# Attention scores from a split in natural layout, in six 64-row matmuls for each step, and the last 64 keys in plain float32

## The chip, the cores and the metric

One core of a Trainium2 chip runs the whole program in one launch. The metric is the device time of one execution in microseconds (us). The kernel before took 601.89 us (median of three runs, 601.4 to 602.93).

## What is computed

```python
def _attn_ref(q, k, v):                       # 4 batches, 12 heads, 448 tokens, 64 columns
    S = q.shape[2]
    scale = 1.0 / np.sqrt(q.shape[-1])
    scores = scale * np.matmul(q, k.transpose(0, 1, 3, 2)) - np.log(S)
    attn = 1.0 / (1.0 + np.exp(-scores))      # a sigmoid: no sum over the keys
    return np.matmul(attn, v)

# x: the heads side by side, 1792 tokens x 768
# soft mixture of 8 experts with 4 slots each: logits = x @ phi; a softmax over the tokens weighs
# the slots' inputs, relu(slots @ w1[e]) @ w2[e] follows, a softmax over the slots weighs the outputs
# last layer: h = x @ w_in (float64 weights); g = h * cos(h); out = g @ w_out (float64 weights)
```

All inputs but `w_in` and `w_out` are float32.

## The kernel before, in words

The program has three stages: attention with the routing, the experts, and the last layer. Only the first is changed.

The attention goes through 24 pairs of heads (`NP`; six pairs make a batch). Head 0 of a pair lies in rows 0 to 63 of its tiles, head 1 in rows 64 to 127; queries are columns 0 to 447 of `raw`, keys columns 448 to 895. A pair has four **steps** g: three with 128 keys and one with the last 64. The loop over `slots` writes each engine's instructions out by hand, in this order: `scores(i, g)` on TensorE into a tile of two PSUM banks (`ps_s`, two tiles in turn), `squash` (the sigmoid, ScalarE), then `attn_v` for the step two before (`LAG`), then one item of `todo` (transposes of finished tokens, logits, sums of the routing), then what VectorE has to prepare for the next pair. `in_between` fills VectorE with work that nothing waits for at once, by the budgets of `SPARE`: the routing's exponentials (`slow`) and the narrowing of `w_in` from float64 patterns to float32 (`narrow`, four instructions for each of 24 pieces of 512 columns).

A float32 score needs three float16 products: upper keys with upper queries, lower keys with upper queries, upper keys with lower queries. Before, `hi` holds four blocks. In blocks 2 and 3 the upper and lower keys of one head lie one under the other in 128 rows, and in blocks 0 and 1 that head's upper queries stand twice, so one 128-row matmul gives the first two products of a head; a 64-row matmul for each head adds the third:

```python
rows = [(slice(0, P), j) for j in range(2)] + [(top, 0), (bottom, 1)]
```

To bring the parts into place VectorE does a cast (L279), three copies in `cast_keys` (L285 to L287) and three in `cast_queries` (L292, L293) for each pair, and GpSimd (POOL) two subtractions (L280, L281). The last 64 keys of both heads go through one product of 128 rows: `split_v` (VectorE, L254, L255) makes two float32r parts of v on a block diagonal, `split_a` (ScalarE L261, POOL L262) two parts of the weights, and three float32r matmuls (L350) take the place of a float32 one. The very last pair does it in float32 without a split (L347).

SyncE issues every DMA in the order of the code: `load_v` and `load_qk` at g = 1, halves of weights (`load_half`) at g = 2, g = 3 and in most pairs at g = 1. There are 15 slots for weights; more is loaded as pieces of `w_in` are narrowed. After the attention its memory is used again from the first address on, in slots of 8,192 bytes per partition: `a0`, `a1`, `a2`, `ct`, `m4`, `zone`. A load into one waits until what lay there has been used. In order of address the attention's pools are `xt2p`, `rawp`, the even pair's `hi` and `lo`, its v, `vh` and `vl`, the odd pair's `hi` and `lo`, its v, `ap_` (the weights), `xtp`, `xp` (the turned tokens), `midp` (the routing's small tiles).

Of the kernel before, what the change touches and what calls it, by code (L numbers as in the profile page):

```python
# [9 lines left out]
F16 = mybir.dt.float16  # L10
# [10 lines left out]
NP = B * HP  # L21
# [11 lines left out]
# a pair's v: three columns of blocks for each head, and one that the two share  # L33
VW = 7 * D
# slots for half a chunk of weights: from the start on, and after the attention for w_out too
W_SLOTS, A_SLOTS = 15, 3
# so many of the first ones are loaded after the attention as well
LATE = 1
# columns of w_in that become float32 at a time, and how many times a pair of heads
CV = 512  # L40
RATE = 1.15
# how far the attention's second product is behind the first
LAG = 2
# steps of a pair of heads that load half a slot, beside every third and fourth
EXTRA = [(i, 1) for i in range(2, 22)]
# steps between the slots' weights and their use
PAUSES = 5
# microseconds that VectorE has in each of a pair's steps for what nothing waits for
SPARE = 0.4, 0.4, 0.8, 1.0
# the difference of the biases of float64 and float32, 1023 - 127, in the upper eight bits of eleven  # L50
F64_SCALE = 2.0 ** -112
# 2^f for f from -1/2 to 1/2, the powers from the first on
# [7 lines left out]
def fused(ctx: ExitStack, tc: tile.TileContext, qk, vv, phi, w1, w2, w_in, w_out, out):  # L60
# [24 lines left out]
    def own_logits(b):  # L85
        """A batch's, tokens to rows; the last one's where no slots' sums are any more."""
        if b < B - 1:
            return l_all[0:CT, b]
        return s_acc.rearrange("p a f -> p (a f)")[0:CT, DM - P:].rearrange("p (c s) -> p c s", c=NC_T)

    # the weights in the order in which they are used, and where each goes
# [8 lines left out]
    # the work space is filled for the first group of experts, after others that are free sooner  # L100
# [6 lines left out]
    def load_half():  # L107
        """A load of weights in two, that it holds up what the attention needs for less long."""
        if not halves_left:
            halves_left.extend(load_w(2))  # L110
        halves_left.pop(0)()
# [45 lines left out]
    def narrow(a, words, dst, eng=None):  # L157
        """float64 bit patterns (low word, high word) to the float32 of their leading bits."""
        low, high = words[:, :, 0], words[:, :, 1]
        # as a float32, the high word has eight of the eleven bits of the exponent in its own exponent;  # L160
        # less the difference of the biases, what three places to the left are a float32's magnitude is left
# [16 lines left out]
    def exp_weights(pool, b, l):  # L178
        """Softmax over the slots (its maximum is taken off), as [hi, lo, hi, lo] for float32r."""
# [30 lines left out]
    # ------------------------------------------------------------ attention and routing  # L210
    with ExitStack() as at:
        # from the first that is free at the end to the last
# [4 lines left out]
        vp = at.enter_context(tc.tile_pool(name="vp", bufs=1))  # L217
        vh, vl = [vp.tile([P, P], F32R, name=f"v{x}") for x in "hl"]
# [10 lines left out]
        # ahead of what is needed for longer  # L229
        midp.tile([P, S], F32, tag="lc", name="lc")  # L230
# [4 lines left out]
        def load_qk(i):  # L235
            # the second pair's before the first's are done with, where no tokens lie yet
            pool, tag = (xp, "xtok") if i == 1 else (rawp, "raw")
            raw[i] = pool.tile([P, QK], F32, tag=tag, name=f"raw{i}", bufs=2 if i == 1 else 1)
            # the first pair's in two, that the first half is there sooner
            for k in (1, 0) if i == 0 else ():  # L240
                nc.sync.dma_start(out=raw[i][:, k * S:(k + 1) * S], in_=qk[i, :, k * S:(k + 1) * S])
            if i:
                nc.sync.dma_start(out=raw[i], in_=qk[i])
# [5 lines left out]
        def split_v(i):  # L249
            """The last 64 rows of two heads, each in its own block, in two parts for float32r."""  # L250
            for j in range(2):
                js = slice(j * D, (j + 1) * D)
                v = v32[i][js, 6 * D:]
                nc.vector.tensor_copy(vh[js, js], v)  # L254
                nc.vector.tensor_sub(vl[js, js], v, vh[js, js].bitcast(F32))  # L255

        def split_a(i):
            """The last of a pair's weights in two parts for float32r."""
            one = aa[i, 3]
            a = aa[i, 3] = ap_.tile([P, 2, S], F32R, tag="a", name=f"ar{i}")  # L260
            nc.scalar.copy(a[:, 0], one)  # L261
            nc.gpsimd.tensor_sub(a[:, 1], one, a[:, 0].bitcast(F32))  # L262

        def block(i, k):
            """Queries of two heads, then keys of two heads."""
            return hi[i][:, k * S:(k + 1) * S]

        def new_pair(i):
            hi[i] = pairs[i % 2].tile([P, 4 * S], F16, tag="hi", name=f"hi{i}")
            lo[i] = pairs[i % 2].tile([P, S], F16, tag="lo", name=f"lo{i}")  # L270
# [3 lines left out]
        def cast(i):  # L274
            """Both heads' upper parts where only one of them stays, and what the keys' leave."""
            new_pair(i)
            r = raw.pop(i)
            both = hi[i].rearrange("p (a k s) -> p a k s", a=2, k=2)
            nc.vector.tensor_copy(both[:, :, 0], r.rearrange("p (a s) -> p a s", a=2))  # L279
            nc.gpsimd.tensor_sub(block(i, 1), r[:, S:], block(i, 2))  # L280
            nc.gpsimd.tensor_sub(lo[i], r[:, 0:S], block(i, 0))  # L281

        def cast_keys(i):
            """The lower part of each head's keys under its upper one."""
            nc.vector.tensor_copy(block(i, 3)[bottom], block(i, 2)[bottom])  # L285
            nc.vector.tensor_copy(block(i, 2)[bottom], block(i, 1)[top])  # L286
            nc.vector.tensor_copy(block(i, 3)[top], block(i, 1)[bottom])  # L287

        def cast_queries(i):
            """Each head's upper part of the queries twice."""  # L290
            for half in (top, bottom):
                nc.vector.tensor_copy(block(i, 1)[half], block(i, 0)[bottom])  # L292
            nc.vector.tensor_copy(block(i, 0)[bottom], block(i, 0)[top])  # L293

        def first_casts():
            new_pair(0)
            q, k = raw[0][:, 0:S], raw.pop(0)[:, S:]
            nc.vector.tensor_copy(block(0, 2)[top], k[top])
            nc.scalar.copy(block(0, 3)[bottom], k[bottom])
            nc.vector.tensor_sub(block(0, 2)[bottom], k[top], block(0, 2)[top])  # L300
            nc.scalar.copy(block(0, 0)[top], q[top])
            nc.vector.tensor_copy(block(0, 0)[bottom], q[top])
            nc.scalar.copy(block(0, 1)[bottom], q[bottom])
            nc.vector.tensor_sub(lo[0][top], q[top], block(0, 0)[top])  # L304
            nc.scalar.copy(block(0, 1)[top], q[bottom])
            nc.gpsimd.tensor_sub(lo[0][bottom], q[bottom], block(0, 1)[bottom])
            nc.vector.tensor_sub(block(0, 3)[top], k[bottom], block(0, 3)[bottom])

        def scores(i, g):
            """The keys' two parts with the queries' upper one, then the upper part with the lower."""  # L310
            ps = ps_s.tile([P, 2, 512], F32, tag="sc", name=f"sc{i}_{g}")
            rows = [(slice(0, P), j) for j in range(2)] + [(top, 0), (bottom, 1)]
            # the very first of them head by head, as they come
            for at, j in rows if i or g else rows[0::2] + rows[1::2]:
                upper = at.stop - at.start == P
                keys, q = block(i, 2 + j)[at], block(i, j) if upper else lo[i][at]
                if g < 3:
                    o, kk = ps[:, j, 0:S], keys[:, g * P:(g + 1) * P]
                else:
                    o, kk = ps[j * D:(j + 1) * D, 0, 0:S], keys[:, g * P:g * P + D]  # L320
                nc.tensor.matmul(o, kk, q, start=upper, stop=not upper)  # L321
# [15 lines left out]
        def attn_v(i, g):  # L337
# [3 lines left out]
            for j in range(2):  # L341
# [4 lines left out]
                elif i == NP - 1:  # L346
                    nc.tensor.matmul(av[i][js, 0:S], v32[i][js, 6 * D:], a[js], start=False, stop=True)  # L347
            if g == 3:
                for v, x in ((vh, 0), (vl, 0), (vh, 1)) if i < NP - 1 else ():
                    nc.tensor.matmul(av[i][:, 0:S], v, a[:, x], start=False, stop=x == 1)  # L350
# [8 lines left out]
        def route(i):  # L359
            """Tokens of one pair of heads to rows; logits once a batch has all its pairs."""  # L360
# [13 lines left out]
            if hp == 2:  # L374
                # ahead of what waits, that there is room for the next pair
# [4 lines left out]
            if hp == HP - 1:  # L380
# [3 lines left out]
                else:  # L384
                    # something that the array has left to do while the maximum is on its way
# [5 lines left out]
        def logits(b, half):  # L391
            """Three pairs of heads side by side, each in its own columns of the array."""
# [8 lines left out]
        def warm_up(n, what=ident):  # L401
            """Products for nothing, that the array's clock is up when something comes."""
# [727 lines left out]
```

## Time and profile before

| | |
|---|---|
| median of three runs | 601.89 us |
| span of the profiled execution | 601.1 us |
| busy in the span: TensorE (PE), VectorE (DVE), ScalarE (ACT), POOL | 544.4, 410.4, 291.6, 140.8 us |
| moved by DMA | 98.14 MB, 162 GB/s on average over the span |
| attention, experts, last layer | about 0 to 226, 226 to 305, 305 to 601 us |

The profile lists one execution. The time of the runs also holds what lies around the span. A matmul's duration in the rows includes the time in which it drains; how fast a series runs is read from one start to the next. PEclk is the granted clock of TensorE as a share of full speed: 1.0 is 2.4 GHz, 0.5 is 1.2 GHz, and a value between is a mean over both. The chain of waits and the waits of an engine tell what it stood still for.

### The profile page before, as it was taken

The page shows a single profiled execution, that of the slowest core. Times are in us where ns is not written, and L with a number is a line of the kernel's source. Part 1 is how long each engine was busy: PE and PEld are TensorE (multiplying, and loading weights), DVE is VectorE, ACT ScalarE, POOL GpSimd, SP SyncE. Part 2 cuts the span into 40 slices and gives each one's busy share as a digit, 9 for nine tenths or more (in the row PEclk, how much of TensorE's full clock was granted, in tenths as well). Part 3 has the DMA queues.
Part 4 walks back from the last instruction along what each step waited for, and adds up shares of the span by engine and source line. Part 5 has one row for each costly group of instructions (what it writes and reads, how often), then busy time and mean ns, then how long its engine had stood idle before and what let it go on. Part 6 is the DMA issues. An engine that isn't in the chain of part 4 may idle for free.

```text
span 601.1 us, 8006 instructions
## 1 busy us (share of the span) xinstructions
PE 544.4 (91%) x2943; PEld 327.4 (54%) x2943; DVE 410.4 (68%) x786; ACT 291.6 (49%) x471; POOL 140.8 (23%) x114
## 2 busy tenths in 40 slices
PE   8999898979898999777988777888999999999997
PEld 3332223223232353222246565656999999999996
DVE  5899989798999822410039999997655655565553
ACT  5877656655665731100036666645444544444442
POOL 3444424323343300000017566561000000000000
PEclk8999989889898999997999989999999999999999
DMA  6688786773642499999974343302000200020002
GB/s 198 212 300 295 250 279 220 243 256 121 216 162 89 168 318 384 386 385 375 348 263 158 105 151 113 130 28 92 1 0 1 93 0 1 1 93 0 1 1 93
DMA packets 46247, 98.14 MB, mean 163 GB/s; under 512 B 2944, under 2 KB 17664, under 8 KB 46208
## 3 DMA queue, kind: packets, MB, share of 16 engines
q1 hardware_dynamic: 46208, 97.63, 47.1%
q8 instruction: 23, 0.38, 0.3%
q14 instruction: 16, 0.13, 0.1%
HBM read 92.11 MB, written 5.51 MB: 162 GB/s over the span
## 4 chain that ended last, share of the span: by engine, by line
PE 54%; DVE 33%; DMA 4%; issue 4%; SPq 3%; ACT 1%; DVEq 0%; ACTq 0%
PE o L1005 29%; PE sc L321 7%; PE av L345 6%; DVE wf L169 5%; DVE wi L965 4%; DMA w<-in_w 4%; SPq L142 3%; DVE hi L285 2%; PE h L746 2%; DVE hi L286 2%; DVE wf L172 2%; PE av L350 2%; DVE hi L292 2%; DVE wi L172 2%; PE h L951 2%
## 5 line engine op out<-in xcount | busy, mean ns | idle before, releaser
L1005 PE MATMUL o<-gh,wh 128*128 128x448 f32 x384 | 128.9, 367 | 10.2 <-ACT gh L989 9.0
L1005 PE MATMUL o<-gh,wl 128*128 128x448 f32 x384 | 131.4, 374 | 2.7 <-POOL wl L910 2.6
L1005 PE MATMUL o<-gl,wh 128*128 128x448 f32 x384 | 129.7, 369 | 2.5 <-POOL gl L990 2.4
L332 ACT ACTIVATE a<-sc,bias_s 128x896 f32<-128x896 f32 x96 | 87.7, 914 | 63.5 <-PE sc L321 58.8
L975 ACT ACTIVATE wi<-wi 128x448 f32<-128x448 f32 x64 | 37.0, 578 | 108.3 <-DVE wi L970 76.0
L1005 PEld LDWEIGHTS o<-gh,wh 128*128 128x128 f32 x384 | 71.1, 188 | 19.3 <-ACT gh L989 12.4
L1005 PEld LDWEIGHTS o<-gh,wl 128*128 128x128 f32 x384 | 72.7, 192 | 13.4 <-POOL wl L910 7.8
L1005 PEld LDWEIGHTS o<-gl,wh 128*128 128x128 f32 x384 | 72.0, 190 | 11.4 <-POOL gl L990 7.0
L321 PEld LDWEIGHTS <-hi 64*128 64x128 f16 (+3 forms) x384 | 21.8, 99 | 100.1 <-issue 73.7
L345 PE MATMUL av<-a,v 128*64 128x448 f32 x288 | 74.3, 596 | 0.0
L321 PE MATMUL sc<-hi 128*128 128x448 f16 x192 | 52.3, 381 | 17.0 <-DVE hi L293 15.5
L990 DVE TENSOR_TENSOR gl<-wi,gh 128x448 fp32r<-128x448 f32 x49 | 31.9, 651 | 42.8 <-ACT gh L989 42.8
L981 DVE TENSOR_TENSOR wi<-h,wi 128x448 f32<-128x448 f32 x64 | 39.7, 621 | 29.0 <-ACT wi L975 29.0
L953 ACT ACTIVATE wi<-h 128x448 f32<-128x448 f32 x64 | 34.6, 541 | 21.6 <-PE h L951 21.3
L262 POOL TENSOR_TENSOR ar<-a,ar 128x448 fp32r<-128x448 f32 x23 | 28.4, 1235 | 66.2 <-ACT ar L261 66.2
L910 POOL TENSOR_TENSOR wl<-wf,wh 128x768 fp32r<-128x768 f32 (+2 forms) x17 | 33.3, 1958 | 36.6 <-ACT wh L906 36.6
L280 POOL TENSOR_TENSOR hi<-raw,hi 128x448 f16<-128x448 f32 x23 | 25.9, 1126 | 56.9 <-DVE hi L279 40.4
L989 ACT CAST gh<-wi 128x448 fp32r<-128x448 f32 x64 | 35.8, 560 | 5.6 <-DVE wi L981 5.4
L321 PE MATMUL sc<-lo,hi 64*128 64x448 f16 x192 | 37.2, 381 | 0.3 <-DVE lo L304 0.3
L788 PE MATMUL so<-w,zone 128*32 128x512 f32 (+1 forms) x256 | 27.6, 523 | 8.6 <-DMA w<-in_w 8.6
L970 DVE TENSOR_TENSOR wi<-wi 128x448 f32<-128x448 f32 x48 | 30.0, 625 | 1.7
L169 DVE SCALAR_TENSOR_TENSOR wf<-wo,wf 128x768 uint32<-128x768 uint32 x16 | 29.4, 1836 | 0.5
(176 smaller groups left out, 713.1 us busy)
## 6 DMA issues: line engine op xcount, KB each, us to landing
w<-in_w SPq DMA_DIRECT2D x25, 1024.0 KB, 14.3
w<-in_w SPq DMA_DIRECT2D x44, 512.0 KB, 6.9
wi<-in_w_in SPq DMA_DIRECT2D x24, 512.0 KB, 6.6
wo<-in_w_out SPq DMA_DIRECT2D x16, 768.0 KB, 4.3
raw<-in_qk SPq DMA_DIRECT2D x23, 448.0 KB, 3.3
v<-in_vv SPq DMA_DIRECT2D x24, 224.0 KB, 3.6
out_t<-wi SPq DMA_DIRECT2D x24, 224.0 KB, 2.1
zone<-in_w SPq DMA_DIRECT2D x1, 1024.0 KB, 8.5
```

The costliest lines, as they stand in the source:

```text
L169: lambda: nc.vector.scalar_tensor_tensor(out=t, in0=low, scalar=29, in1=t, op0=ALU.logical_shift_right, op1=ALU.bitwise_or),
L321: nc.tensor.matmul(o, kk, q, start=upper, stop=not upper)
L332: nc.scalar.activation(a, ps, AF.Sigmoid, bias=bias_s, scale=qk_scale)
L345: nc.tensor.matmul(av[i][js, 0:S], v32[i][:, vc:vc + D], a[:, j], start=g == 0, stop=False)
L910: nc.gpsimd.tensor_sub(wl[:, f, cols], wf[f][:, cols], wh[:, f, cols].bitcast(F32))
L953: nc.scalar.activation(ph, h, AF.Copy, bias=0.25, scale=inv2pi)
L970: nc.vector.tensor_sub(ph, tn, ph)
L975: nc.scalar.activation(tn, ph, AF.Sin, scale=-2.0 * math.pi)
L981: nc.vector.tensor_mul(g, hs.pop(u), tn)
L989: nc.scalar.copy(gh, g)
L990: (nc.gpsimd if u < NF - 1 else nc.vector).tensor_sub(gl, g, gh.bitcast(F32))
L1005: nc.tensor.matmul(ps, w[:, f, o * P:(o + 1) * P], g, start=f == 0 and w is wh and g is gh, stop=f == NF - 1 and g is gl,)
```

## The change

Parts are split where they lie. `hi` and `lo` are two tiles of the shape of `raw` (896 columns each); head 0 stays in the upper 64 rows, head 1 in the lower. One cast and one subtraction on VectorE fill them, at g = 0 and g = 1. Each step's scores are six 64-row matmuls, the three products for head 0 and head 1 in turn. The last 64 keys go through two float32 matmuls of 64 rows by 64 columns in all pairs. `split_v`, `split_a`, `cast_keys`, `cast_queries` and POOL's part of the splits are gone. The first instruction of a piece of `w_in` is always VectorE's (before, ScalarE did 22 of 24), and `SPARE` is larger. Comments that were taken out are not shown.

```diff
-SPARE = 0.4, 0.4, 0.8, 1.0
+SPARE = 0.8, 0.4, 1.3, 1.2
...
-        vp = at.enter_context(tc.tile_pool(name="vp", bufs=1))
-        vh, vl = [vp.tile([P, P], F32R, name=f"v{x}") for x in "hl"]
...
         def new_pair(i):
-            hi[i] = pairs[i % 2].tile([P, 4 * S], F16, tag="hi", name=f"hi{i}")
-            lo[i] = pairs[i % 2].tile([P, S], F16, tag="lo", name=f"lo{i}")
+            hi[i] = pairs[i % 2].tile([P, QK], F16, tag="hi", name=f"hi{i}")
+            lo[i] = pairs[i % 2].tile([P, QK], F16, tag="lo", name=f"lo{i}")
...
+        def cast_upper(i):
             new_pair(i)
+            nc.vector.tensor_copy(hi[i], raw[i])
+        def cast_lower(i):
+            nc.vector.tensor_sub(lo[i], raw.pop(i), hi[i])
         def first_casts():
+            nc.vector.tensor_copy(hi[0][:, k], r[:, k])
+            nc.scalar.copy(hi[0][:, q], r[:, q])
+            nc.vector.tensor_sub(lo[0][:, k], r[:, k], hi[0][:, k])
+            nc.vector.tensor_sub(lo[0][:, q], r[:, q], hi[0][:, q])
         def scores(i, g):
             ps = ps_s.tile([P, 2, 512], F32, tag="sc", name=f"sc{i}_{g}")
+            h, l = hi[i], lo[i]
+            terms = [(h, h), (l, h), (h, l)]
+            for n, (keys, q) in enumerate(terms):
+                for j, at in enumerate((top, bottom)):
+                    o = ps[:, j, 0:S] if g < 3 else ps[j * D:(j + 1) * D, 0, 0:S]
+                    kk = keys[at, S + g * P:min(S + (g + 1) * P, QK)]
+                    nc.tensor.matmul(o, kk, q[at, 0:S], start=n == 0, stop=n == len(terms) - 1)
...
-                elif i == NP - 1:
+                else:
                     nc.tensor.matmul(av[i][js, 0:S], v32[i][js, 6 * D:], a[js], start=False, stop=True)
...
-                if g == 3 and i < NP - 1:
-                    split_a(i)
-                if g == 0 and due(i):
-                    narrow_piece(None)
...
-                if more and g in (1, 2):
-                    (cast_keys, cast_queries)[g - 1](i + 1)
...
-                if more and g == 0:
-                    cast(i + 1)
-                if i < NP - 1 and g == 3:
-                    split_v(i)
+                if more and g < 2:
+                    (cast_upper, cast_lower)[g](i + 1)
```

TensorE, the step g = 1 of the second pair and the product for the first pair's last keys. Before (`sc` are the scores, `ar` the split weights, `vh` and `vl` the parts of v):

```order
L321 LDWEIGHTS hi_179
L321 MATMUL sc_1_246<-hi_179 128x448
L321 LDWEIGHTS hi_179
L321 MATMUL sc_1_246<-hi_179 128x448
L321 LDWEIGHTS hi_179
L321 MATMUL sc_1_246<-lo_180,hi_179 128x448
L321 LDWEIGHTS hi_179
L321 MATMUL sc_1_246<-lo_180,hi_179 128x448
L350 MATMUL av_208<-ar_220,vh 128x448
L350 MATMUL av_208<-ar_220,vl 128x448
L350 MATMUL av_208<-ar_220,vh 128x448
```

The same place now:

```order
L279 LDWEIGHTS hi_169
L279 MATMUL sc_1_228<-hi_169 128x448
L279 LDWEIGHTS hi_169
L279 MATMUL sc_1_228<-hi_169 128x448
L279 LDWEIGHTS lo_170
L279 MATMUL sc_1_228<-hi_169,lo_170 128x448
L279 LDWEIGHTS lo_170
L279 MATMUL sc_1_228<-hi_169,lo_170 128x448
L279 LDWEIGHTS hi_169
L279 MATMUL sc_1_228<-lo_170,hi_169 128x448
L279 LDWEIGHTS hi_169
L279 MATMUL sc_1_228<-lo_170,hi_169 128x448
L305 MATMUL av_195<-a_3_207,v_137 64x448 x2
```

Two 128-row and two 64-row matmuls became six of 64 rows, head 0 and head 1 in turn, and three matmuls over both heads became two over one head each.

VectorE, the work for one pair. Before (`sl` are sums for the slots):

```order
L279 CAST hi_883<-raw_829 128x2x448
L169 SCALAR_TENSOR_TENSOR wi<-wi_1_1_381,wi 128x512
L285 COPY hi_883<-hi_883 64x448
L286 COPY hi_883<-hi_883 64x448
L287 COPY hi_883<-hi_883 64x448
L519 COPY s_acc<-sl_0_904 128x384
L519 COPY run_z<-sl_0_904 128x1
L172 SCALAR_TENSOR_TENSOR wi<-wi_1_1_381,wi 128x512
L292 COPY hi_883<-hi_883 64x448 x2
L293 COPY hi_883<-hi_883 64x448
```

Now:

```order
L256 CAST hi_990<-raw_934 128x896
L163 TENSOR_SCALAR wi<-wi_2_1_459 128x512
L168 TENSOR_SCALAR wi<-wi 128x512
L259 TENSOR_TENSOR lo_991<-raw_934,hi_990 128x896
L169 SCALAR_TENSOR_TENSOR wi<-wi_2_1_459,wi 128x512
L172 SCALAR_TENSOR_TENSOR wi<-wi_2_1_459,wi 128x512
```

The copies are gone, one subtraction has come, and a piece of `w_in` begins on VectorE.

SyncE, the loads into the attention's own memory at its end, with what each waits for (engines, and DMAHW for earlier loads; `w_1_1_1` goes to `a0`, `w_1_2_0` to a slot for weights, then `a1`, `a2`, `ct`, `m4`, `zone`). Before:

```order
L130 DMA w_1_2_0_2311<-in_w 128x4x512 [waits DVE_49,Activation_49]
L130 DMA w_1_2_1_2313<-in_w 128x4x512 [waits DMAHW1_49,DVE_49,PE_49]
L130 DMA w_1_3_0_2315<-in_w 128x4x512 [waits DMAHW5_49,PE_49,Activation_49]
L130 DMA w_1_3_1_2317<-in_w 128x4x512 [waits PE_49,Activation_49,Pool_49]
L130 DMA w_1_4_0_2319<-in_w 128x4x512 [waits DMAHW3_49,PE_49,Activation_49]
L130 DMA zone<-in_w 128x4x512 [waits DMAHW4_49,DVE_49,PE_49]
```

Now:

```order
L130 DMA w_1_2_0_2145<-in_w 128x4x512
L130 DMA w_1_2_1_2147<-in_w 128x4x512 [waits DMAHW1_49,DMAHW5_49,PE_49,Activation_49]
L130 DMA w_1_3_0_2149<-in_w 128x4x512 [waits Activation_49]
L130 DMA w_1_3_1_2151<-in_w 128x4x512 [waits PE_49,Activation_49]
L130 DMA w_1_4_0_2153<-in_w 128x4x512 [waits DMAHW3_49,PE_49]
L130 DMA zone<-in_w 128x4x512 [waits DVE_49,DMAHW4_49,PE_49,Activation_49]
```

The order is the same; since the even and odd tiles and `vp` take 2,816 bytes less below them, the later pools lie lower, and each slot covers other tiles than before.

## Rows read from the trace of the kernel before

**Rows 1.** Busy time of each engine, PEclk, DMA share and GB/s: two parts of the attention, and a stretch of the experts. Columns: stretch, its length, then PE, PEld (weight loads), DVE, ACT, POOL busy with the number of instructions, PEclk, DMA share, GB/s.

```profile
12.00:72.00 60.00, 57.04 (x294) 18.55 (x294) 53.41 (x112) 44.61 (x62) 26.79 (x24) 1.00 0.79 265
72.00:212.00 140.00, 126.89 (x663) 41.00 (x657) 122.61 (x296) 87.22 (x121) 49.52 (x44) 0.91 0.58 195
240.00:260.00 20.00, 15.63 (x136) 5.50 (x132) 9.26 (x34) 2.68 (x4) 0.00 (x0) 1.00 1.05 386
```

**Rows 2.** The same view of four single pairs, each from its last step's first matmul to that of the next pair.

```profile
11.47:18.42 6.95, 6.95 (x37) 2.22 (x34) 3.98 (x11) 5.20 (x7) 3.31 (x3) 1.00 0.37 120
40.21:47.74 7.53, 7.03 (x36) 2.33 (x35) 7.03 (x15) 5.78 (x8) 3.26 (x3) 1.00 0.89 318
100.17:112.73 12.56, 10.12 (x38) 2.62 (x37) 9.27 (x21) 5.89 (x8) 4.30 (x4) 0.73 0.78 264
127.50:141.25 13.75, 10.77 (x55) 2.68 (x51) 12.31 (x37) 5.70 (x8) 4.77 (x5) 0.75 0.70 235
```

**Rows 3.** The waits of TensorE from 0 to 207 us, the longest group: us in total, times, longest us.

```profile
PE sc L321 <- DVE hi L293: 15.5, 9, 3.0
```

**Rows 4.** TensorE in order of time in a pair without waits: start us, duration us, line, tiles, number of instructions.

```profile
18.42 0.38 PE L321 MATMUL sc<-hi 128*64 128x448 f16 x2
18.73 0.38 PE L321 MATMUL sc<-lo,hi 64*64 64x448 f16 x2
19.04 0.97 PE L345 MATMUL av<-a,v 128*64 128x448 f32 x4
19.94 0.55 PE L321 MATMUL sc<-hi 128*128 128x448 f16 x2
20.43 0.36 PE L321 MATMUL sc<-lo,hi 64*128 64x448 f16 x2
20.72 0.97 PE L345 MATMUL av<-a,v 128*64 128x448 f32 x4
...
22.40 0.47 PE L350 MATMUL av<-ar,vh 128*128 128x448 f32 x1
22.71 0.36 PE L350 MATMUL av<-ar,vl 128*128 128x448 f32 x1
22.91 0.37 PE L350 MATMUL av<-ar,vh 128*128 128x448 f32 x1
23.12 0.36 PE L321 MATMUL sc<-hi 128*128 128x448 f16 x1
```

**Rows 5.** The chain of waits, single pieces: start us, us on the chain, what. `lg` are logits, `sl` sums for the slots, `lt` the totals, and L347 is the float32 product for the last pair's last 64 keys.

```profile
83.30 0.88 PE lg L396 x6
85.70 0.83 PE sl L536 x8
215.42 0.90 PE av L347 x4
216.32 0.89 PE lt L420 x8
```

**Rows 6.** The routing's transposes on TensorE, in order of time.

```profile
178.14 0.43 PE L447 MATMUL tl<-ident,td 64*112 64x64 f32 x4
```

**Rows 7.** Busy time from 11.47 to 212.05 us of the instructions that touch one tile: first `hi`, then `vh`. Columns for `hi`: PE, PEld, DVE, ACT, POOL; for `vh`: PE, PEld, DVE.

```profile
11.47:212.05 200.58, 78.59 (x368) 20.55 (x366) 81.05 (x154) 0.00 (x0) 47.95 (x44) 0.94 0.65 216
11.47:212.05 200.58, 20.53 (x46) 9.33 (x46) 25.13 (x92) 0.94 0.65 216
```

**Rows 8.** Groups of instructions: line, engine, operation, tiles, shapes, number | busy us, mean ns of one | idle us before them, and what ended it.

```profile
L788 PE MATMUL so<-w,zone 128*32 128x512 f32 (+1 forms) x256 | 27.6, 523 | 8.6 <-DMA w<-in_w 8.6
L285 DVE COPY hi<-hi 64x448 f16<-64x448 f16 x23 | 22.4, 973 | 0.7
L279 DVE CAST hi<-raw 128x896 f16<-128x896 f32 x23 | 15.2, 659 | 0.9 <-DMA raw<-in_qk 0.3 <-PE sc L321 0.3
L165 ACT ACTIVATE wi<-wi 128x512 f32<-128x512 f32 x22 | 14.6, 662 | 0.0
L168 DVE TENSOR_SCALAR wi<-wi 128x512 uint32<-128x512 uint32 x24 | 11.0, 457 | 4.3 <-ACT wi L165 3.9
L287 DVE COPY hi<-hi 64x448 f16<-64x448 f16 x23 | 6.3, 273 | 0.7
```

**Rows 9.** The first pair, ScalarE and VectorE in order of time.

```profile
3.41 0.39 DVE L298 CAST hi<-raw 64x448 f16<-64x448 f32 x1 [1.07 <-DMA raw<-in_qk]
3.83 0.62 DVE L300 TENSOR_TENSOR hi<-raw,hi 64x448 f16<-64x448 f32 x1
3.99 0.56 ACT L301 CAST hi<-raw 64x448 f16<-64x448 f32 x1
7.55 1.01 ACT L332 ACTIVATE a<-sc,bias_s 128x896 f32<-128x896 f32 x1 [1.82 <-PE sc L321]
```

**Rows 10.** The end of the attention: issues of loads on SyncE's queue (into `a1`, `a2`, `m4` and `zone`), and VectorE's last instruction for the routing.

```profile
212.78 0.37 SPq L130 DMA_DIRECT2D w<-in_w  x1
216.40 0.37 SPq L130 DMA_DIRECT2D w<-in_w  x1
222.06 0.37 SPq L130 DMA_DIRECT2D w<-in_w  x1
222.73 0.37 SPq L130 DMA_DIRECT2D zone<-in_w  x1
226.66 0.29 DVE L483 TENSOR_TENSOR s_acc<-s_acc,cm 112x128 f32<-112x128 f32 x1
```

More of the change, by code (lines that the diff above doesn't have):

```diff
@@ L227, in fused @@
         ps_m = at.enter_context(tc.tile_pool(name="ps_m", bufs=1, space=PSUM))
-        midp.tile([P, S], F32, tag="lc", name="lc")
+        zeros = midp.tile([P, S], F32, tag="lc", name="zeros")[:, 0:P]
         fold = midp.tile([P, NS], F32, name="fold")
@@ L247, in load_v @@
             nc.sync.dma_start(out=v32[i], in_=vv[i])
[L249 to L262, printed above, removed]
@@ L264, in block @@
-        def block(i, k):
-            return hi[i][:, k * S:(k + 1) * S]
         def new_pair(i):
-            hi[i] = pairs[i % 2].tile([P, 4 * S], F16, tag="hi", name=f"hi{i}")
-            lo[i] = pairs[i % 2].tile([P, S], F16, tag="lo", name=f"lo{i}")
+            hi[i] = pairs[i % 2].tile([P, QK], F16, tag="hi", name=f"hi{i}")
+            lo[i] = pairs[i % 2].tile([P, QK], F16, tag="lo", name=f"lo{i}")
         top, bottom = slice(0, D), slice(D, P)
-        def cast(i):
+        def cast_upper(i):
@@ L276, in cast @@
             new_pair(i)
[L277 to L293, printed above, removed]
+            nc.vector.tensor_copy(hi[i], raw[i])
+        def cast_lower(i):
+            nc.vector.tensor_sub(lo[i], raw.pop(i), hi[i])
         def first_casts():
             new_pair(0)
[L297 to L307, printed above, removed]
+            q, k = slice(0, S), slice(S, QK)
+            r = raw.pop(0)
+            nc.vector.tensor_copy(hi[0][:, k], r[:, k])
+            nc.scalar.copy(hi[0][:, q], r[:, q])
+            nc.vector.tensor_sub(lo[0][:, k], r[:, k], hi[0][:, k])
+            nc.vector.tensor_sub(lo[0][:, q], r[:, q], hi[0][:, q])
@@ L309, in scores @@
         def scores(i, g):
             ps = ps_s.tile([P, 2, 512], F32, tag="sc", name=f"sc{i}_{g}")
[L312 to L321, printed above, removed]
+            h, l = hi[i], lo[i]
@@ L345, in attn_v @@
                     nc.tensor.matmul(av[i][js, 0:S], v32[i][:, vc:vc + D], a[:, j], start=g == 0, stop=False)
-                elif i == NP - 1:
+                else:
                     nc.tensor.matmul(av[i][js, 0:S], v32[i][js, 6 * D:], a[js], start=False, stop=True)
             if g == 3:
-                for v, x in ((vh, 0), (vl, 0), (vh, 1)) if i < NP - 1 else ():
-                    nc.tensor.matmul(av[i][:, 0:S], v, a[:, x], start=False, stop=x == 1)
                 if i == NP - 1:
@@ L621, in fused @@
         with tc.manual_schedule():
-            for x in (vh, vl):
-                nc.vector.memset(x.bitcast(U32), 0)
-            warm_up(8, vh.bitcast(F32))
+            nc.vector.memset(zeros, 0.0)
+            warm_up(8, zeros)
             load_qk(0)
```

## The prediction

> **What bounds the kernel now.** I read the stretches first, then single pairs, then TensorE's waits, then the order of time inside a pair. From 12 to 72 us TensorE is busy for 57.0 of 60 us and VectorE for 53.4; from 72 to 212 us it is 126.9 and 122.6 of 140, with PEclk at 0.91 [rows 1]. Two engines that are both at about nine tenths call for a pair at a time. The second pair takes 6.95 us, all of it TensorE; a later one takes 7.53 with VectorE at 7.03, and two at the ends of batches take 12.56 and 13.75 with PEclk at 0.73 and 0.75 [rows 2]. The wait is named: nine times, 15.5 us in all and 3.0 at the longest, the scores wait for L293, VectorE's last copy of the next pair's parts [rows 3]. So the attention is TensorE's when VectorE is in time, VectorE's otherwise, and after a long wait TensorE goes on at a lower granted clock (a mean of 0.73 is a mixture of 1.2 and 2.4 GHz) and pays again.
>
> How much that is: take the first pair's last step at 11.47 us and the last pair's at 212.05 (the two ends of the stretch in [rows 7]). Without waits and at full clock, 23 pairs would take 23 x 6.95 = 159.9 us. To that come the routing's matmuls that this pair has none of: seven halves of logits at 0.88, and for three batches 0.89 for the totals, 0.43 for the transposes and twice 0.83 for the sums [rows 5, 6], 6.2 + 3 x 2.98 = 15.1 us. 11.47 + 159.9 + 15.1 = 186.5, against 212.05: **25.6 us** are waits and low clock.
>
> **The change, part by part.**
>
> *Scores, steps of 128 keys.* In the pair without waits a step takes from 19.94 to 20.72, 0.78 us [rows 4]: the two 128-row matmuls are 0.19 apart (0.55 for both, 0.36 for one), and 0.49 after the first the 64-row pair starts in another shape, 0.29 before what follows. That pair is two matmuls in 0.36, what one takes, so the two heads' rows do run side by side. Now there are three such pairs in one shape. The last takes 0.29 as before; for the two ahead I take 0.20 each, the distance of L350's matmuls with new weights [rows 4]. 0.70 us, 0.08 less; at 0.19 it would be 0.67. If new weights waited, each would take the 0.29 or more that a change of shape costs; that is a rival below.
>
> *Scores, last step.* 18.42 to 19.04, 0.62 us [rows 4], for two pairs; now three, 0.70: 0.08 more. *Last 64 keys.* Three float32r matmuls take 22.40 to 23.12, 0.72 us [rows 4]. The float32 form stands in the trace at the last pair, 0.90 [rows 5]: 0.18 more, in 23 pairs. Together a pair has -3 x 0.08 + 0.08 + 0.18 = +0.02 us on TensorE, 0.5 us over 23 pairs. **TensorE gains nothing of its own**; the change is worth what VectorE no longer delays.
>
> *VectorE.* What touches `hi` took 81.05 us and `split_v` 25.13 [rows 7], 106.2 of some 176.0 us [rows 1]. In their place come, for each of 22 pairs, a cast like L279's (0.66 with POOL's interference [rows 8]) and one subtraction of 896 columns: between 0.62, which 448 columns took, and 1.24, twice that [rows 9]; I take 1.1, since elements and not the fixed part make most of it. The first instruction of 22 pieces moves over from ScalarE; VectorE's L168 of the same shape takes 0.46 [rows 8]. 176.0 - 106.2 + 22 x (0.66 + 1.1 + 0.46) = 118.6 us, in a stretch that would now be about 175: 68%. The larger `SPARE` changes where this stands, not how much it is. At the end of a batch the subtraction stands behind the maximum and its four followers; it is needed two whole steps later (2 x (0.70 + 0.90) = 3.2 us), where before the last copies had one. POOL's subtractions also cost VectorE time: L285 is the same copy as L287 and takes 973 ns instead of 273 [rows 8]. That goes with them.
>
> *ScalarE* loses 22 casts of 0.66 us [rows 8] and `split_a`. Neither is on the path, as it was busy for 131.8 of 200 us [rows 1]; I cost this at nothing, and it would cost nothing with ScalarE as full as before. *SyncE's queue* no longer waits for POOL or `split_v`; each `raw` is issued after the subtraction, three steps ahead of its use. The same bytes in less time: 265 GB/s over 60 us [rows 1] become about 305, and a pair at 318 GB/s went by already [rows 2]. If that cover were gone, the 386 GB/s of [rows 1] would be the limit, and it lies above.
>
> *Start.* The first sigmoid began at 7.55 us. The keys' cast at 3.41 (0.39), the queries' on ScalarE from 3.99 (0.56) and a subtraction of 0.62 behind it [rows 9] end at 5.2; a matmul of 0.36 [rows 4] and 0.1 more, 5.65: 1.9 us earlier.
>
> *Experts.* They live on DMA (386 GB/s [rows 1], and the products wait 8.6 us for it [rows 8]), so they move with the end of the attention, less what the loads lose. Memory below the slots is 2,816 bytes smaller, so slot `a1` now reaches into the odd pair's v, which is read up to the last product: its load, issued at 212.78, goes to about where that of `a2` was, 216.40. `zone` now covers all of `midp` and waits for the routing's last subtraction, 226.66 + 0.29 instead of 222.73 [rows 10]; `ct` and `m4` move by one place in the same row. In a queue that is otherwise full this leaves one transfer too few: 1,048,576 bytes at 386 GB/s, 2.7 us lost. The bounds are 0 (the gap was there anyway) and 5.4 (two transfers).
>
> *Sum:* 25.6 + 1.9 - 0.5 - 2.7 = 24.3 us off the profiled span of 601.1, 576.8. The median of the runs is 0.8 above that span, so **577.6 us**. Its own range: 1 us for the start, 2.7 for steps of 0.67 (96 x 0.03 = 2.9) and 2.7 for the loads down to 571; up to 6 us of waits that stay, 584. About 0.3%, 1.8 us, is what a measurement of this kernel can tell from no change.
>
> **Rivals.**
>
> *A: waits stay at the ends of batches.* VectorE's exponentials and the subtraction share one queue, and a single long wait brings the lower clock with it. Half of 25.6 stays: 590 us. For it speaks that the two worst pairs are such ends [rows 2], against it the 57 us that VectorE gains.
>
> *B: new weights wait for the matmul of the same rows.* Then the second and third pairs cost 0.30 rather than 0.20, 96 x 2 x 0.10 = 19.2 us: 597 us. The float16 rows speak against it: two 128-row matmuls with their own weights are 0.19 apart [rows 4], so there the second load does not wait. But no row has two 64-row matmuls in turn in the same rows. The Trainium skill (TensorE: Matmul & The Clock Gate, Part 3, "The mechanism") says that a weight load overlaps a running matmul only where the row group differs; by that rule the time would be that of this rival. On full rows the trace disagrees with it.
>
> *C: slower.* In 64-row shape a matmul starts only when the one before it in the same rows has drained: 0.36 [rows 4] and some 0.10 for the weights (0.29 - 0.19), 0.46 a pair, 1.38 a step. Against the 0.70 above that is 96 x 0.68 = 65 us: 643 us. From 0.70 + (601.9 - 577.6) / 96 = 0.95 us a step on, the kernel would be slower than before. For it speaks that no row shows otherwise in this shape, against it that no shape in the trace does so.
>
> *D: VectorE stays the bound,* so that nothing changes: 602 us. It would need about 175 us of work where I count 119.
>
> **How the numbers follow.** Forecast 0.66, A 0.11, B 0.09, C 0.08, D 0.04, and 0.02 for a time below 571 (a shorter end of the attention). A's end at 590 and the waits around it reach to 594; forecast and A make 0.77, with some of B's lower part 0.8: 571 to 594. Faster by over 0.3%: 0.66 + 0.11 + 0.09 + 0.02 = 0.88. Within: D, 0.04. Slower: C, 0.08.
>
> **What would show it.** In the profile after: no wait of the scores for VectorE above 0.5 us, pairs of 6.9 to 7.0 us all along, PEclk at 1.0 until the end of the attention, VectorE at about two thirds there, POOL empty, a step of 0.67 to 0.72 us, the last pair's last step near 185 us, `zone` issued after the routing's last subtraction. Steps of 0.9 us and more, or pairs still at 12 us at batch ends, would make it wrong; so would an attention that ends early and experts that don't.

## The result, and the profile after

The changed kernel took **574.81 us** (median of four runs, 574.51 to 575.84; four runs of the kernel before beside them: 601.91). The ratio is 0.9554, 95% interval 0.9528 to 0.9581: 27 us less, inside the forecast range and 2.8 us below its number. The profiled span fell from 601.1 to 572.9 us. One run of all that follow, of the kernel with the subtraction on POOL, took 658.68 us at a granted clock of 0.75; the ratios leave it out.

The stretches of the attention first, then all of it from the first pair's last step to the last pair's, then a part of the experts (columns as in [rows 1]):

```profile
12.00:72.00 60.00, 60.00 (x402) 17.42 (x400) 34.88 (x67) 37.65 (x49) 0.00 (x0) 1.00 0.86 286
72.00:182.00 110.00, 110.00 (x744) 33.02 (x744) 71.14 (x163) 67.56 (x88) 0.00 (x0) 1.00 0.69 237
8.70:181.82 173.12, 173.12 (x1165) 51.27 (x1163) 106.70 (x231) 106.85 (x138) 0.00 (x0) 1.00 0.75 254
230.00:250.00 20.00, 14.50 (x84) 4.08 (x75) 0.00 (x0) 0.59 (x1) 0.00 (x0) 0.70 1.05 387
```

From 12 us on TensorE is busy without a gap and at full clock to the end of the attention, where [rows 1] had 126.9 of 140 us and 0.91. VectorE went from nine tenths to 107 of 173 us, POOL to nothing. TensorE's waits from 0 to 190 us, all of them, against [rows 3]:

```profile
PE idle L361 <- DVE zeros L578: 1.0, 1, 1.0
PE sc L279 <- ACT a L290: 0.5, 1, 0.5
```

Both lie in the first pair's start; no score waits for VectorE any more. TensorE in order of time from one pair's last step (15.59) to the next pair's (22.48), against [rows 4]:

```profile
15.59 0.38 PE L279 MATMUL sc<-hi 64*64 64x448 f16 x2
...
17.18 0.36 PE L279 MATMUL sc<-hi 64*128 64x448 f16 x2
17.38 0.35 PE L279 MATMUL sc<-hi,lo 64*128 64x448 f16 x2
17.57 0.35 PE L279 MATMUL sc<-lo,hi 64*128 64x448 f16 x2
17.85 0.97 PE L303 MATMUL av<-a,v 128*64 128x448 f32 x4
...
19.43 0.97 PE L305 MATMUL av<-a,v 64*64 64x448 f32 x4
20.33 0.36 PE L279 MATMUL sc<-hi 64*128 64x448 f16 x2
...
22.48 0.38 PE L279 MATMUL sc<-hi 64*64 64x448 f16 x2
```

A step of 128 keys takes 17.18 to 17.85, 0.67 us: pairs of heads 0.20 and 0.19 apart, 0.28 behind the last. The group with the last 64 keys takes 0.90, the last step 0.69 (22.48 to 23.17), and the whole pair 6.89 us (6.95 before).

VectorE's groups from 8 to 190 us, which answer to [rows 8]:

```profile
L259 DVE TENSOR_TENSOR lo<-raw,hi 128x896 f16<-128x896 f32 x23 | 24.9, 1082 | 0.0
L172 DVE SCALAR_TENSOR_TENSOR wi<-wi,wi 128x512 uint32<-128x512 uint32 x24 | 16.6, 690 | 0.7
L256 DVE CAST hi<-raw 128x896 f16<-128x896 f32 x22 | 13.8, 626 | 42.7 <-DMA raw<-in_qk 42.7
L168 DVE TENSOR_SCALAR wi<-wi 128x512 uint32<-128x512 uint32 x24 | 10.2, 427 | 0.8
```

New is the 42.7 us in which VectorE stands at the cast until `raw` has come in. The first pair's start, against [rows 9], one row each of VectorE and ScalarE:

```profile
4.56 0.62 DVE L268 TENSOR_TENSOR lo<-raw,hi 128x448 f16<-128x448 f32 x1
6.06 1.91 ACT L290 ACTIVATE a<-sc,bias_s 128x896 f32<-128x896 f32 x2 [1.53 <-PE sc L279]
```

And the end of the attention, SyncE's issues (into `a1`, then `zone`) and VectorE's last subtraction, against [rows 10]:

```profile
186.23 0.37 SPq L130 DMA_DIRECT2D w<-in_w  x1
196.94 0.37 SPq L130 DMA_DIRECT2D zone<-in_w  x1
196.50 0.29 DVE L439 TENSOR_TENSOR s_acc<-s_acc,cm 112x128 f32<-112x128 f32 x1
```

`a1`'s load goes out 4.41 us behind the last pair's last step (181.82), where that of `a2` was (216.40 - 212.05 = 4.35), and `zone`'s when the subtraction ends, both as forecast; before, `zone` went out 4 us ahead of it.

Over the whole span: the first pair's last step comes 2.77 us earlier (8.70 for 11.47), the time from there to the last pair's is 27.46 us shorter (173.12 for 200.58), and what follows is 2.03 us longer (391.08 for 389.05). 2.77 + 27.46 - 2.03 = 28.2.

### The profile page after: what moved, and what is told of

Same layout as the page of the kernel before. It is cut to its first block, busy times and chain, and to the rows that moved or that the text cites. A ratio compares the mean times of both kernels' runs of the same rounds, so it can differ in the third digit from the quotient of the medians.

```text
span 572.9 us, 8039 instructions
## 1 busy us (share of the span) xinstructions
PE 534.5 (93%) x3158; PEld 319.1 (56%) x3158; DVE 337.0 (59%) x598; ACT 264.8 (46%) x423; POOL 61.4 (11%) x44
## 4 chain that ended last, share of the span: by engine, by line
PE 72%; DVE 16%; DMA 4%; SPq 4%; issue 2%; POOL 1%; ACT 1%; POOLq 0%; DVEq 0%
PE o L952 31%; PE av L303 11%; PE sc L279 11%; DVE wf L169 5%; DVE wi L912 4%; DMA w<-in_w 4%; PE av L305 4%; PE h L693 3%; SPq L142 3%; PE xn L325 2%; DVE wf L172 2%; PE h L898 2%; DVE wf L168 2%; DVE wi L928 1%; PE idle L361 1%
## 5 line engine op out<-in xcount | busy, mean ns | idle before, releaser
L303 PE MATMUL av<-a,v 128*64 128x448 f32 x288 | 70.0, 565 | 0.0
L279 PEld LDWEIGHTS <-hi 64*128 64x128 f16 (+1 forms) x384 | 20.0, 97 | 60.8 <-issue 48.8
L256 DVE CAST hi<-raw 128x896 f16<-128x896 f32 x23 | 14.4, 626 | 44.5 <-DMA raw<-in_qk 44.5
L735 PE MATMUL so<-w,zone 128*32 128x512 f32 (+1 forms) x256 | 29.8, 561 | 8.6 <-DMA w<-in_w 8.5
L279 PE MATMUL sc<-hi 64*128 64x448 f16 x192 | 35.8, 365 | 0.5 <-ACT a L290 0.5
L279 PE MATMUL sc<-hi,lo 64*128 64x448 f16 x192 | 34.5, 351 | 0.0
L279 PE MATMUL sc<-lo,hi 64*128 64x448 f16 x192 | 34.5, 351 | 0.0
L163 POOL TENSOR_SCALAR wf<-wo 128x768 f32<-128x768 f32 x1 | 2.2, 2248 | 282.1 <-PE h L898 282.1
## 6 DMA issues: line engine op xcount, KB each, us to landing
w<-in_w SPq DMA_DIRECT2D x25, 1024.0 KB, 14.1
```

The costliest lines, as they stand in the source:

```text
L279: nc.tensor.matmul(o, kk, q[at, 0:S], start=n == 0, stop=n == len(terms) - 1)
L303: nc.tensor.matmul(av[i][js, 0:S], v32[i][:, vc:vc + D], a[:, j], start=g == 0, stop=False)
L735: nc.tensor.matmul(e2[g, k][j * NS:(j + 1) * NS, 0:n], h1[g][:, c + a, j * NS:(j + 1) * NS], w[:, a, j], start=c + a == 0, stop=c + a == F ...
```

## The experiments

Ratios are to runs of the kernel before on the same chip.

**The change once more.** 

> The changed kernel once more, beside the kernels of the same series. Every theory expects 574.8 us, 0.955 of the kernel before.

575.52 us (574.71 to 575.9), 0.9574 (0.9549 to 0.9599): the same. But here TensorE waits once, at the end of a batch, for the routing's sums, which VectorE adds up; that pair takes 10.18 us where the other ends of batches take 8.84:

```profile
PE xn L325 <- DVE s_acc L471: 1.3, 1, 1.3
```

**VectorE's load taken off the kernel before.** Three of the four narrowing instructions of each piece of `w_in` are left out in the attention, so the last layer gets other numbers.

```diff
-            pending.extend(narrow(a, w[:, o:o + CV], a, eng))
+            narrow(a, w[:, o:o + CV], a, eng)
+            pending.extend(3 * [lambda: None])
```

> The kernel before, which leaves out three of four instructions for each piece of w_in in the attention (w_in keeps wrong values): VectorE has some 2.0 us less to do for each pair, 131 of 176 us stay; scores, copies and POOL's part are as before the change. Theory (VectorE was late, nothing else): no or few waits for L293, pairs near 6.95 us, PEclk near 1.0, the last pair's last step near 187 to 190 us, 576 to 580 us. Rival (the gain comes from the 64-row steps, from float32 or from POOL's absence): 595 us or more.

577.98 us (576.62 to 581.04), 0.9619 (0.9592 to 0.9645). From 12 to 72 us, and the longest group of waits:

```profile
12.00:72.00 60.00, 58.27 (x290) 18.66 (x287) 34.91 (x91) 43.68 (x60) 25.66 (x24) 0.97 0.78 263
PE sc L321 <- DVE hi L293: 1.6, 2, 1.4
```

The old scores, the old POOL work and the old memory, but VectorE as free as in the change (34.91 against 34.88 us): 23 of the 27 us (its own runs of the kernel before took 601.17 us, and 601.17 - 577.98 = 23.2) come without any change on TensorE. The time is inside the 576 to 580 expected; the last pair's last step, at 191.2 us, is a little behind the 187 to 190. What the change was worth is, for the most part, VectorE's lateness.

**Memory.** In the changed kernel, 2,816 bytes of filler put every later tile at its old address.

```diff
+        vp = at.enter_context(tc.tile_pool(name="vp", bufs=1))
+        zeros = vp.tile([P, 704], F32, name="zeros")[:, 0:P]
         pairs.append(at.enter_context(tc.tile_pool(name="odd", bufs=1)))
...
-        zeros = midp.tile([P, S], F32, tag="lc", name="zeros")[:, 0:P]
+        midp.tile([P, S], F32, tag="lc", name="lc")
```

> The changed kernel with 2,816 bytes of filler between the even and the odd pair's tiles, so that the slots at the attention's end cover the tiles that they covered before. Theory (the experts live on DMA, and two loads start later than they could): the load into slot a1 starts after the last pair's scores, some 4 us earlier against the end of the attention, zone some 4 us earlier, and the whole is 2.0 to 2.7 us faster than the changed kernel, 572.1 to 572.8 us. Rival (the gap was there anyway, the products catch up): 574.8 within 0.5. Rival (the places matter for something else in the attention): the last pair's last step is not at 182 us.

572.01 us (571.28 to 573.57), 0.9523 (0.9499 to 0.9547); no kernel of the study is faster. A stretch of the changed kernel, then the same with the filler, and there the issues into `a1` and `zone`:

```profile
182.00:186.00 4.00, 4.00 (x22) 0.84 (x18) 0.62 (x1) 2.63 (x4) 0.00 (x0) 1.00 0.05 17
```

```profile
182.00:186.00 4.00, 4.00 (x22) 0.84 (x18) 0.62 (x1) 2.62 (x4) 0.00 (x0) 1.00 0.51 188
182.60 0.37 SPq L130 DMA_DIRECT2D w<-in_w  x1
192.55 0.37 SPq L130 DMA_DIRECT2D zone<-in_w  x1
```

The attention is the same to the instruction (last pair's last step 181.81 for 181.82 us). Only the loads differ: 17 GB/s while `a1` waits becomes 188, `a1`'s load goes out 3.6 us earlier and `zone`'s 4.4, and the run is 3.5 us shorter than the changed kernel beside it on the same chip (575.52), 2.8 shorter than in the first series (574.81). The forecast of 2.7 us was for this.

**A weight load moved ahead,** in the kernel with filler (`LATE` 1 to 0, `RATE` 1.15 to 1.35), to fill the rest of the hole. 

> same_addresses with w_in narrowed sooner (RATE 1.35 instead of 1.15) and with the last of the 15 slots loaded in the attention (LATE 0 instead of 1), where DMA has room, and not behind it. Theory (the experts live on DMA from the attention's end on): one transfer of 1 MiB less there, 2.7 us faster than same_addresses' 572.0, 569.3 us. Rival (VectorE's or DMA's denser work makes TensorE wait): 572 us or more, with waits in the attention.

572.32 us (571.05 to 574.19), 0.9537 (0.9513 to 0.956): no gain, a miss. The stretch ahead of the hole, and the hole:

```profile
178.00:182.00 4.00, 4.00 (x25) 0.96 (x24) 0.00 (x0) 3.29 (x4) 0.00 (x0) 1.00 0.60 232
182.00:186.00 4.00, 4.00 (x24) 1.25 (x26) 0.62 (x1) 2.86 (x5) 0.00 (x0) 1.00 0.31 95
```

With filler alone the two had 393 and 188 GB/s: the hole only grew, since the load into `a1` still goes out 0.8 us behind the last pair's last step (183.25 and 182.46; with filler alone 182.60 and 181.81), and the memory that it waits for is no sooner free. That step itself comes 0.65 us later, and TensorE waits 1.0 us for the routing's sums at the end of a batch, which is in part what the rival said.

**The old product for the last 64 keys** (`split_v`, `split_a` and three float32r matmuls back in), with the same memory. 

> The same with filler, and with the last 64 keys as before the change: split_v on VectorE, split_a on ScalarE and POOL, three float32r matmuls of 0.72 us in place of two float32 ones of 0.90. Theory (the attention is TensorE's alone): 23 x 0.18 = 4.1 us faster than same_addresses, about 568.5 us, the last pair's last step near 178 us, no wait of TensorE for VectorE or POOL. Rival (POOL's work on the shared memory and VectorE's splits bring the waits back): not faster than same_addresses, 572 us or more, with waits of the av matmuls for vl or ar in the trace.

572.03 us (571.09 to 573.38), 0.9524 (0.9497 to 0.955): a miss, no gain over 572.01. TensorE in order, then its longest waits for VectorE:

```profile
25.60 0.47 PE L326 MATMUL av<-ar,vh 128*128 128x448 f32 x1
...
26.40 0.36 PE L297 MATMUL sc<-hi 64*128 64x448 f16 x2
PE xn L345 <- DVE s_acc L491: 1.2, 2, 0.6
PE av L326 <- DVE vh L255: 0.5, 1, 0.5
```

The group takes 25.60 to 26.40, 0.80 us and not the 0.72 of [rows 4], because 64-row scores now follow it and the change of shape costs about 0.1 (0.29 for 0.20). That leaves 0.10 a pair, 2.3 us. TensorE's waits for VectorE at the ends of batches take 1.9 of it back (1.4 us in all for the routing's sums, 0.5 for `vh`), so that the time from the first pair's last step to the last pair's is only 0.3 us shorter (172.76 for 173.07). So the rival held in kind, though most of the waiting is for the routing's sums and not for the split parts that it named.

**The order of the heads.** Three products of head 0, then three of head 1, instead of the heads in turn.

```diff
-            for n, (keys, q) in enumerate(terms):
-                for j, at in enumerate((top, bottom)):
+            for j, at in enumerate((top, bottom)):
+                for n, (keys, q) in enumerate(terms):
```

> The changed kernel with each step's six matmuls in another order: the three products of head 0, then the three of head 1. Theory (two matmuls run side by side only where neighbours in the program lie in different rows, and starts are in order): five starts 0.19 apart and 0.29 behind the last, with only one pair side by side, 1.05 us a step instead of 0.67, 96 x 0.38 = 36 us more, about 611 us. Rival (TensorE takes matmuls of the other rows ahead by itself, or the two heads never ran side by side): a step stays as it is and so does the time, 575 us.

575.16 us (two runs), 0.9571 (0.953 to 0.9612): a complete miss for the theory. TensorE's matmuls of one step, and a row of its weight loads:

```profile
17.26 0.37 PE L279 MATMUL sc<-hi 64*128 64x448 f16 x2
17.27 0.11 PEld L279 LDWEIGHTS <-lo 64*128 64x128 f16 x2
17.46 0.36 PE L279 MATMUL sc<-hi,lo 64*128 64x448 f16 x2
17.65 0.36 PE L279 MATMUL sc<-lo,hi 64*128 64x448 f16 x2
```

The program has head 1's first product behind head 0's third, the rows have the two heads' first products together. Most likely the engine pairs them itself. The rows hold start times, not the order in which the instructions reached the engine, so it is not shown that no step of the build put the heads in turn. Against that speaks that each pair now takes 6.92 us instead of 6.89 (15.66 to 22.58): the engine got another program than with the heads in turn.

**The subtraction on POOL.** 

> The changed kernel with the subtraction for the lower parts on POOL (one of 896 columns, some 2.2 us for each pair) instead of VectorE. Theory (what counts is only that the parts are there in time): 574.8 us within 1, although VectorE's other instructions take longer beside POOL's. Rival (POOL's interference was itself the price): slower than the changed kernel by 3 us or more, with TensorE waiting for lo or for VectorE.

574.57 us, 0.9568 (0.9545 to 0.9592): the same time, as the theory said. But VectorE, rid of 24.9 us of subtractions, is busy for longer:

```profile
8.70:181.66 172.96, 172.96 (x1162) 51.15 (x1160) 117.50 (x208) 106.80 (x138) 45.37 (x23) 1.00 0.76 254
L168 DVE TENSOR_SCALAR wi<-wi 128x512 uint32<-128x512 uint32 x24 | 32.2, 1342 | 0.8
```

L168 takes 1,342 ns on average beside POOL instead of 427. No score waits for VectorE or for `lo`.

**How much room VectorE has.** Cast and subtraction are done twice each (some 39 us more on VectorE).

```diff
-            nc.vector.tensor_copy(hi[i], raw[i])
+            for _ in range(2):
+                nc.vector.tensor_copy(hi[i], raw[i])
...
-            nc.vector.tensor_sub(lo[i], raw.pop(i), hi[i])
+            for _ in range(2):
+                nc.vector.tensor_sub(lo[i], raw[i], hi[i])
+            raw.pop(i)
```

> The changed kernel with each pair's cast and subtraction on VectorE done twice over (same result), some 22 x 1.7 = 37 us more work for VectorE in the attention, 80 to 85% busy instead of about 60%. Theory (the attention is TensorE's, VectorE has slack): 574.8 us within 2, the last pair's last step near 182 us, at most a few waits at the ends of batches. Rival (VectorE's work counts one to one, or a third of it): 587 to 612 us.

589.12 us (588.86 to 589.49), 0.9812 (0.9791 to 0.9833): a miss by 14 us, inside the rival's range, with VectorE still idle for a sixth and more of each stretch (89.8 of 108 us busy from 72 to 180, 42.1 of 60 from 12 to 72). TensorE's and VectorE's longest waits:

```profile
PE sc L282 <- DVE lo L261: 9.3, 11, 1.4
DVE hi L257 <- DMA raw<-in_qk: 27.9, 15, 3.6
```

TensorE waits for VectorE while VectorE waits for `raw`. To tell volume from place, the next two add as much work, two additions on a scratch tile for each pair, at two places of the kernel with filler: ahead of the subtraction, as here, or behind `in_between`.

```diff
+                if more and g == 1:
+                    for _ in range(2):
+                        nc.vector.tensor_add(scratch, scratch, scratch)
                 if more and g < 2:
                     (cast_upper, cast_lower)[g](i + 1)
                 in_between(i, SPARE[g])
```

*Behind the subtraction.* 

> The kernel same_addresses (572.0 us), and for each pair two additions on VectorE of a scratch tile of 704 float32 columns onto itself (estimated 0.85 us each from the subtraction of 896 columns, 1.08; some 39 us in all, as much as the doubled cast and subtraction of casts_twice), placed right behind the subtraction, in the time in which VectorE would stand at the next cast waiting for raw. Theory 'raw's round trip' (one buffer: cast, subtraction, next load some 4 us, all in turn; what is doubled on that loop made casts_twice slow, not VectorE's volume): nothing on the loop is longer, so 571 to 574 us, pairs at 6.9 and no waits of the scores of over 1 us in all. Rival 'volume' (VectorE has no more than some 30 us to give away, whatever the place): 586 to 590 us, with the scores waiting for the subtraction some 9 us as in casts_twice.

577.9 us (574.76 to 579.7), 0.9593 (0.9534 to 0.9651): between the two.

*Ahead of it.* 

> The same two additions for each pair as in work_behind, placed right ahead of the subtraction, so that raw's next load is issued 1.7 us later. Theory 'raw's round trip': landing 4.1, cast 0.63, two narrowing instructions 0.85, additions 1.7, subtraction 1.08 make 8.4 us with raw in use or under way, more than a pair's 6.9; 584 to 590 us, with waits of the scores for the subtraction as in casts_twice (9.3 us). Rival 'volume': the same 586 to 590, and work_behind the same as this. Third: neither place matters, since casts_twice was slow by the doubled cast alone (it holds up the subtraction of the same tile): 572 to 575 us here too.

585.82 us (585.37 to 587.59), 0.9744 (0.9703 to 0.9785). TensorE's waits, behind, and a stretch after the longest of them:

```profile
PE xn L328 <- DVE s_acc L474: 2.4, 2, 1.6
PE xn L328 <- DVE s_acc L478: 2.3, 1, 2.3
80.04:83.30 3.26, 3.26 (x14) 1.25 (x14) 3.19 (x6) 1.40 (x2) 0.00 (x0) 0.50 0.92 293
```

And ahead, with VectorE's and SyncE's rows around the longest of them, and two stretches behind long waits:

```profile
PE sc L282 <- DVE lo L262: 6.6, 7, 2.3
44.53 1.08 DVE L262 TENSOR_TENSOR lo<-raw,hi 128x896 f16<-128x896 f32 x1
45.65 0.33 SPq L244 DMA_DIRECT2D raw<-in_qk  x1
51.82 0.63 DVE L259 CAST hi<-raw 128x896 f16<-128x896 f32 x1 [4.87 <-DMA raw<-in_qk]
53.16 1.81 DVE L620 TENSOR_TENSOR zeros<-zeros 128x704 f32<-128x704 f32 x2
54.89 1.08 DVE L262 TENSOR_TENSOR lo<-raw,hi 128x896 f16<-128x896 f32 x1
57.53:60.95 3.42, 3.42 (x14) 0.64 (x14) 1.56 (x4) 1.70 (x3) 0.00 (x0) 0.50 0.88 263
132.65:139.40 6.75, 6.21 (x21) 2.06 (x22) 6.58 (x12) 3.06 (x4) 0.00 (x0) 0.50 0.85 300
```

The same work costs 5.9 us at one place and 13.8 at the other against 572.01, which was taken on another chip; by the ratios it is 4 and 13 us. The runs behind scatter from 574.76 to 579.7, but all lie below those ahead. Ahead, it lies on a loop: subtraction done at 45.6, `raw` issued at 45.65, in at 51.8, cast, additions, subtraction done at 56.0. That is 10.3 us for a pair that needs 6.9, with one buffer for `raw` and a landing that took 6.2 us here; the loop ahead of it had taken 7.7 (issue at 37.87). Such loops use up the two steps in hand, and the scores wait 2.3 us. Of the seven waits, 6.6 us in all, this is the only one without a batch's routing in VectorE's queue close ahead of it; the other six have the routing's maxima or sums there, in the same pair or the one before, so loop and queue add up in them. Behind, no score waits for a subtraction, as this theory said; but the time is not the 571 to 574 it gave. At batch ends the routing's sums come late in the same queue, and three ends take 3.9, 1.6 and 0.9 us longer. Waits and clock account for both times: 4.7 us of waits and half of 3.4 us at a granted clock of 0.50 behind, 9.0 and half of 10.2 ahead, are 6.4 and 14.1 us (an estimate, from rows in which a product takes 1.72 us at a granted clock of 0.50 and 0.97 at 1.00), and the time from the first pair's last step to the last pair's grew by 6.4 and 15.2. So place decides over volume for the larger part, and the queue's order at batch ends for the rest. That the loop, and not the later subtraction by itself, makes the scores wait is read from the rows above; no run shows it. A second buffer for `raw` would test it. It takes 3,584 bytes for each partition, 768 more than the 2,816 that the change gave back, and wasn't tried.

## Why the prediction was right

*What bounds the kernel: right.* The 25.6 us of waits and low clock were VectorE's. They are gone in the change, and a kernel with the old scores gains 23 us when only the narrowing is left out of it.

*The pair on TensorE: right in kind, 0.08 us too long.* Forecast 6.97, measured 6.89. The three steps are 0.67 and not 0.70, since the pairs are 0.19 to 0.20 and 0.28 apart; the last step (0.69 for 0.70) and the last 64 keys (0.90) came as said. 23 x 0.08 = 1.8 us. With the routing at 14.65 for 15.1 (181.82 - 8.70 - 23 x 6.89) the stretch came to 173.1 for 175.4.

*VectorE: 107 us for 119, the term that was mis-sized most.* Cast and subtraction came to 0.63 and 1.08 for 0.66 and 1.1. Most of what was missed is POOL's price in instructions that the change doesn't touch: L172 fell from 880 to 690 ns (24 times, 4.6 us), L168 from 457 to 427, and the routing's small ones fell too (`l_all` from 822 to 291 ns, three times). That adds up to some 8 of the 12 us, and cast, subtraction and the first instruction of a piece (0.42 for 0.46) to 2 more; the rest was not followed. That POOL is the cause is borne out in the run with the subtraction on it, where L172 is back at 821 ns. None of it was on the path. But rival D took it that VectorE bounds the kernel only from about 175 us of work on, and the experiments show that this is not so: some 40 us more, about 145 in all, cost 4 to 14 us, by place.

*Start: 2.77 us for 1.9.* The first sigmoid came at 6.06, later than the 5.65 forecast. The subtraction ends at 5.18, as said, but the first three pairs of matmuls take 0.54 to 0.58 us instead of 0.35; those are the times of the lower clock (0.56 for such a pair at 9.44 us in the kernel before), though the view gives 1.00 there, so this cause is not shown. From the sigmoid to the last step it took 2.64 us and not 3.92. In the kernel before most of that stretch ran at a granted clock of 0.50, and its first product took 1.72 us (0.97 now); the sum began to count low clock only at 11.47 and left this out:

```profile
8.61:11.47 2.86, 2.86 (x8) 0.69 (x9) 2.28 (x6) 1.85 (x2) 1.35 (x2) 0.50 0.96 312
```

In the change it is 1.00 from 7.12 to 8.70.

*Loads: 2.03 us for 2.7 in the trace,* 2.8 to 3.5 us by the kernel with filler. The mechanism is shown: the slots cover other tiles. *Sum:* 0.9 + 1.8 + 0.5 + 0.7 make the span 3.9 us shorter than the 576.8 forecast; the median lies 1.9 above the span and not 0.8, which takes 1.1 back.

*ScalarE and SyncE's queue: right in kind.* TensorE's only wait for ScalarE is the 0.5 us at the start, and DMA moved 286 GB/s in the first stretch (forecast 305, and 265 before); no score waits for it.

*The rivals.* A: the ends of batches are 8.84 to 8.89 us long with the routing's matmuls in them, and nothing waits there in the profiled run. It is not far, though: in the repetition one end waits 1.3 us, and work at the wrong place brings just these waits back. B and C: two products in the same 64 rows with new weights are 0.19 to 0.20 us apart, as on full rows, and the weights of the second product are loaded 0.01 us after the first has started (17.27 and 17.26 in the rows of the order of the heads). The rule of the Trainium skill behind B (TensorE: Matmul & The Clock Gate, Part 3, "The mechanism"), that a weight load overlaps a running matmul only where the row group differs, is not what these rows show. The same section says that matmuls start strictly in the order of the program; the run with the heads apart disagrees, if the order of kernel.py is what reached the engine. D: VectorE has 66 us without work.

## What to carry to other kernels

When two engines are both near nine tenths, look for the one that the other waits for, and ask what a change frees on that one; what it does to the other's instruction count may be worth nothing. An idle share is not room: find the loop that the idle time belongs to (here, as the rows read, a single buffer's load, cast, subtraction), and place work off it. A change of a tile's size moves all that lies above it in memory, and loads that reuse the memory later then wait for other tiles: keep the addresses, or choose them.

## What the runs showed of the hardware

- TensorE runs matmuls of different 64-row halves side by side even where kernel.py has them three instructions apart: pairs start 0.19 to 0.20 us apart in either order (575.16 us, and 575.52 for the heads in turn on the same chip).
- A change of matmul shape costs about 0.1 us in these rows: 0.28 to 0.29 where the shape changes, 0.19 to 0.20 where only the weights do.
- POOL's subtraction more than undoes what it takes from VectorE: 24.9 us moved away, and VectorE's busy time rose from 106.7 to 117.5.
- In the experts, which wait for DMA, the granted clock fell to 0.70, a mean of 1.2 and 2.4 GHz, in a stretch with TensorE busy for 14.5 of 20 us; DMA moved 387 GB/s there. The kernel before has 1.00 with 15.6 of 20 us in [rows 1] and 0.86 with 13.7 in the 20 us behind it, both at 386 GB/s. So the clock moves there without a change in the bytes moved.
